# Untiled key products for two batches, a later remainder product in slab 5, and a value cast on VectorE in an attention-plus-MLP kernel

## Chip, cores, metric

One core of one Trainium2 chip. The metric is the device time of one execution in microseconds (us). A kernel's executions differ by some tenths of a per cent; every ratio here is between runs of the fast state (none over 1.5% above the fastest of its kernel), timed in the same rounds on the same chip as the kernel before. A profiled span is some 2 us shorter than the timed execution.

## The reference

Linear attention (softmax of q over the head dimension, softmax of k over the sequence), then a two-layer MLP with a swish whose slope is given per channel. It is 8 batches x 8 heads x 576 tokens x 64, so 4608 rows of 512, and an inner width of 2048.

```python
q_s = softmax(q, axis=-1);  k_s = softmax(k, axis=2)
kv  = einsum('bhsd,bhse->bhde', k_s, v)
x   = einsum('bhsd,bhde->bhse', q_s, kv)       # -> (B*S, H*D)
h   = x @ w_in                                 # 512 -> 2048
out = (h * sigmoid(beta * h)) @ w_out          # 2048 -> 512
```

## The kernel before

A hand-scheduled program. The rows go through in nine slabs of 512: slab b (0 to 7) holds the first 512 tokens of batch b, slab 8 the last 64 tokens ("remainder") of all batches. Each slab has a first pass (x times w_in, 64 matmuls of 512 columns) and a second (times w_out, 112 matmuls of 256 columns after a Strassen-like trick; 64 of 512 in slab 0). The attention of batch b + 1 is threaded between the matmuls of slab b. A counter of steps, 64 a pass, says where: `(step, work)`.

The parts that matter here:

```python
# key-value product of a head pair: column-tiled (two 64-column halves) or not
def tiled(b):
    return b > 1
...
if not tiled(b):
    mm(PS[bk][:, 256 * n:256 * n + VW - 1], l, r_[:, 0:VW - 1], j == 0, j == 4, ...)
for h in range(2) if tiled(b) else ():
    p = slice(64 * h, 64 * h + 64)
    add(PE, lambda e, h=h, p=p: e.matmul(PS[bk][p, ...], l[:, p], ..., tile_position=(0, 64 * h), ...))

# slabs 1 to 3 prepare batches 2 to 4 late in their second pass
def attn_late(b):
    ...
    if b < 4:
        s = [(101, steps(kv_all, b)), (104, lambda: g_diff(1))]
        return s + spread(x[0:2], 117, 120)      # output products: need QT

# queries: normalised on GpSimd, transposed by a DMA that SyncE issues
def norm_turn(b, hp0):  norm_main(b, hp0, 2, POOL); turn(b, hp0, 2)       # -> QT
def norm_turn_rem():    norm_rem(); turn_rem()                            # -> QTR

# remainder output products of slabs 4 to 6: need QTR
todo += spread(outr_steps(2 * t - 5), *((72, 88), (40, 56), (60, 76))[t - 4])

# batch 1, beside slab 0's second pass, in VectorE's order
norm_main(1, 2, 1, DVE)          # sums, reciprocal, multiply: EQ
w_sum(0, 4, 4)                   # half a weight sum: WSUM
norm_main(1, 3, 1, DVE)
w_sum(2, 4, 4)
```

Names in the profile: XT is x of a slab, GT its activations, GS sums of GT, EK and VB the exponentials of keys and the cast values, EKR those of the remainder keys, KVD the normalised key-value blocks (RC is the reciprocal in front of them). SPq is the queue of SyncE, which issues the transfers.

The softmax here doesn't subtract the row's maximum and nothing guards it: scores larger than these inputs give would overflow.

Of the kernel before, what the change touches and what calls it, by code (L numbers as in the profile page):

```python
# [8 lines left out]
ALU = mybir.AluOpType  # L9
AX = mybir.AxisListType  # L10
# [18 lines left out]
PE, ACTE, DVE, POOL, SP = "tensor", "scalar", "vector", "gpsimd", "sync"  # L29
# [13 lines left out]
class Program:  # L43
# [12 lines left out]
    def add(self, eng, fn, r=(), w=(), bank=(), slot=None, after=(), war=False):  # L56
        op = Op(eng, fn, slot)
        op.pos = len(self.ops)
        deps = op.deps
        deps.extend(after)  # L60
        for k in r:
            deps.extend(self.writer.get(k, ()))
            self.readers.setdefault(k, []).append(op)
        for k in w:
            for d in self.readers.get(k, ()):
                if d is not op and (war or not self._same(d, op)):
                    deps.append(d)
            for d in self.writer.get(k, ()):
                if not self._same(d, op):
                    deps.append(d)  # L70
            self.readers[k] = []
            self.writer[k] = [op]
        for k in bank:
            t = self.touch.setdefault(k, {})
            for e, d in t.items():
                if e != eng:
                    deps.append(d)
            t[eng] = op
        if eng == POOL and slot is None:
            if self.pool is not None:  # L80
                deps.append(self.pool)
            self.pool = op
        self.ops.append(op)
        return op
# [71 lines left out]
def bass_efficient_attn_shen__then__act_swish_beta_kernel(  # L156
# [12 lines left out]
    with ExitStack() as es:  # L169
        def sb(name, shape, dt):  # L170
# [52 lines left out]
        add = P.add  # L223
# [6 lines left out]
            r=["ts"], w=["idb"])  # L230
        add(POOL, lambda e: e.tensor_scalar(IDF[:, :], TS[0:NF, 0:NF], 0.0, None, ALU.is_equal),
            r=["ts"], w=["idf"])
        add(ACTE, lambda e: e.dma_start(BT[:, :], bass.AP(beta_h, 0, [[128, NF], [1, 128]])),
            w=["bt"], slot="bt")
        add(ACTE, lambda e: e.activation(DUMMY[:, 0:1], WARM[:, 0:1], ACT.Exp), r=["warm"],
            w=["dummy"])
# [91 lines left out]
            add(ACTE, lambda e: e.activation(EQR[:, :, :], QRF[:, :, :], ACT.Exp),  # L328
                r=[("qrf", 0), ("qrf", 1)], w=["eqr"])

        def norm_main(b, hp0, n, eng=DVE):
            i = b % 2
            a = bass.AP(EQ[i], hp0 * 512, [[2048, 128], [64, 8 * n], [1, 64]])
            s_ = bass.AP(QS[i], hp0 * 8, [[32, 128], [1, 8 * n]])
            v_ = bass.AP(QI[i], hp0 * 8, [[32, 128], [1, 8 * n]])
            vb = bass.AP(QI[i], hp0 * 8, [[32, 128], [1, 8 * n], [0, 64]])
            ks = [("eq", i, hp) for hp in range(hp0, hp0 + n)]
            add(DVE, lambda e: e.tensor_reduce(s_, a, AX.X, ALU.add), r=ks, w=[("qs", i, hp0)])  # L338
            add(DVE, lambda e: e.reciprocal(v_, s_), r=[("qs", i, hp0)], w=[("qi", i, hp0)])  # L339
            add(eng, lambda e: e.tensor_tensor(a, a, vb, ALU.mult), r=ks + [("qi", i, hp0)],  # L340
                w=ks)

        def norm_rem():
            vb = bass.AP(QRI, 0, [[H, 128], [1, H], [0, 64]])
# [77 lines left out]
            return b if b < 2 else 2 + b % 4  # L422

        def tiled(b):
            return b > 1

        def kvd(b, hp, bk, c):
            i = b % 2
# [52 lines left out]
        def outr_steps(b):  # L481
            pi = b // 2
            st = {}

            def one(hp, e_):
                if hp == 0 and e_ == 0:
                    st["b"] = bank()
                bk = st["b"]
                c = hp * 128 + e_ * 64
                d = kd(2 * pi + e_)  # L490
                mm(PS[bk][:, c:c + 64], KVD[d][:, hp, :], QTR[:, hp, 64 * e_:64 * e_ + 64],
                   True, True, r=[("kvd", d, hp), "qtr"], w=[("ps", bk)], bk=bk)
                if hp == 3 and e_ == 1:
                    o = bass.AP(XT8, pi * 128, [[NM * SM, 128], [SM, NM], [1, 128]])
                    add(DVE, lambda e: e.tensor_copy(o, PS[bk][:, :]), r=[("ps", bk)],
                        w=[("xt8", pi)], bank=[bk])
            return [lambda hp=hp, e_=e_: one(hp, e_) for hp in range(NHP) for e_ in range(2)]
# [22 lines left out]
        def one(fn, *a):  # L520
            return lambda: fn(*a)

        def steps(fn, *a):
            return lambda: go(fn(*a))
# [12 lines left out]
        def attn_late(b):  # L537
            x = []
            for hp in range(NHP):
                x += out_step(b, hp, MB, ACTE if hp % 2 else DVE)  # L540
            if b < 4:
                s = [(101, steps(kv_all, b)), (104, lambda: g_diff(1))]
                return s + spread(x[0:2], 117, 120)
            s = [(96, steps(kv_all, b)), (99, lambda: g_diff(1))]
            return s + spread(x, 107, 123)

        def spread(steps, lo, hi):
            return [(lo + (hi - lo) * k / len(steps), s) for k, s in enumerate(steps)]
# [29 lines left out]
        def load_wout(c):  # L578
# [11 lines left out]
            r=[("ps", bb)], w=["bc0"], bank=[bb])  # L590
        add(DVE, lambda e: e.scalar_tensor_tensor(BC[:, :], PS[bb][:, 0:NF], 1e-20, BC[:, :],
                                                  ALU.is_lt, ALU.mult),
            r=[("ps", bb), "bc0"], w=["bc"], bank=[bb])
# [120 lines left out]
        def g_diff(fh):  # L714
            f, th = NG * fh, 1 - fh
            add(DVE, lambda e: e.tensor_tensor(gv(f, th, NG), gv(f, th, NG), gv(f, 1 - th, NG),  # L716
                                               ALU.subtract),
                r=gk(f, 0, NG) + gk(f, 1, NG), w=gk(f, th, NG), war=True)
# [7 lines left out]
        def w_sum(n, i=0, k=NG):  # L726
            x, y = (((0, 0), (1, 1)), ((0, 0), (0, 1)), ((1, 0), (1, 1)))[n]
            add(DVE, lambda e: e.tensor_tensor(WSUM[n][:, i:i + k, :], quarter(*x)[:, i:i + k, :],  # L728
                                               quarter(*y)[:, i:i + k, :], ALU.add),
                r=wkeys(*x)[i:i + k] + wkeys(*y)[i:i + k],  # L730
                w=[("ws", n, i_) for i_ in range(i, i + k)])
# [127 lines left out]
        for t in range(NSLAB):  # L859
            todo = []  # L860
            if t == 0:
                todo = [(x, steps(t_steps, 1, (hp,), NOW, ACTE))
                        for hp, x in enumerate((97, 106, 114, 119))]
                todo += [(107, one(exp_kr_s, 1))]
                todo += [(x, one(exp_k, 1, hp, 1)) for hp, x in enumerate((108, 115, 120, 125.5))]
                todo += [(x, one(cast_v, 1, hp, DVE if hp else POOL))
                         for hp, x in enumerate((115, 118.5, 123, 127))]
                todo += [(x, steps(kv_steps, 1, (hp,), NOW))
                         for hp, x in enumerate((118, 122, 126))]
                todo += [(x, steps(out_step, 1, hp, NOW, ACTE)) for hp, x in enumerate((121, 125))]  # L870
                todo += [(117, one(o2_evac, 0, 0, 3, ACTE))]
                todo += [(2, steps(out_step, 0, 3, HEAD, DVE))]
            elif t < 4:
                todo = attn_late(t + 1)
                if t > 1:
                    todo += [(1, steps(out_step, t, 2, MB, ACTE)), (2.5, steps(out_step, t, 3))]
                if t == 3:
                    todo += [(4, one(norm_turn, 4, 2))]
                if t == 1:
                    todo += [(1, steps(out_step, 1, 2, (3,), ACTE)),  # L880
                             (3, steps(kv_steps, 1, (3,), (7,))),
                             (6, steps(out_step, 1, 3, (7,), DVE)),
                             (6.1, one(w_diff, 0)), (6.2, one(w_diff, 1))]
            elif t < 7:
                todo = attn(t + 1)
                if t > 3:
                    todo += spread(outr_steps(2 * t - 5), *((72, 88), (40, 56), (60, 76))[t - 4])
            elif t == 7:
                todo = spread(outr_steps(1), 32, 48)
            todo = sorted(todo, key=lambda x: -x[0])  # L890
# [30 lines left out]
            if t == 0:  # L921
                load_main("qf", qt_h, QF, 1, split=4, after=P.writer[("wout", 3, 0)])
                load_rem_s("krf", kt_h, KRF, 1)
                load_rem_s("vrf", vt_h, VRF, 1)
                load_kv(1)
                load(2, rem=False)
                exp_q(1)
                w_sum(0, 0, 4)
                w_sum(2, 0, 4)
                norm_main(1, 0, 1, DVE)  # L930
                norm_main(1, 1, 1, DVE)
                cast_vr_s(1)
                norm_main(1, 2, 1, DVE)
                w_sum(0, 4, 4)
                norm_main(1, 3, 1, DVE)
                w_sum(2, 4, 4)
                pass2_group(0, (0, 1, 2, 3), (3, 4, 5, 6), tick)
                while todo:
                    todo.pop()[1]()
                load(2, main=False)  # L940
                load_rem("qrf", qt_h, QRF, 2)
                add(ACTE, lambda e: e.activation(DUMMY[:, 2:3], WARM[:, 0:1], ACT.Silu),
                    r=["warm"], w=["dummy"])
                load(3)
                continue
# [95 lines left out]
```

## Time and profile before

| | before |
|---|---|
| time, median of 6 runs | 275.14 us (274.56 to 275.44) |
| span of the profiled run | 273.4 us |
| TensorE busy | 263.5 us (96%) |
| TensorE's clock | 0.997 |

To read it: "busy" of TensorE counts modelled matmul ends, so 96% does not mean 96% of its peak, but it does mean that TensorE nearly always has a matmul in hand. What is left to win by reordering is the list of its waits. A wait line names who waited, for which engine or transfer, how long in all, how often, and the longest. The lines are in the prediction.

### The profile page before, as it was taken

The numbers are of one execution on the slowest core, as the hardware profiler recorded it, in microseconds if no ns is written. First come the engines' busy times: TensorE is split into PE (matmuls) and PEld (weight loads), VectorE is DVE, ScalarE is ACT, GpSimd is POOL, SyncE is SP. The second block draws the span as 40 slices with busy tenths as digits, with TensorE's granted clock in tenths as the row PEclk, the third lists the DMA queues.
The fourth block names the chain that finished last, engine by engine and source line by source line (L and its number), as shares of the span: only waits on it lengthen the run. The fifth ranks groups of instructions, "written<-read, shape, count | busy, mean of one in ns | idle before, by whom it ended". The sixth has DMA issues, their size and how long they took to land.

```text
span 273.4 us, 4889 instructions
## 1 busy us (share of the span) xinstructions
PE 263.5 (96%) x1921; PEld 164.1 (60%) x1945; DVE 194.5 (71%) x415; ACT 181.0 (66%) x284; POOL 64.3 (24%) x81
## 2 busy tenths in 40 slices
PE   8899999999999999999999998999999999999994
PEld 3444454448744875478547863587458745874683
DVE  4964586787967799869786977778587549625762
ACT  4897568789288956897778846693783477018610
POOL 2790010006530099000900770036000100000000
PEclk9999999999999999999999999999999999999998
DMA  7999999989699139950499999303600030012005
GB/s 216 317 204 207 228 328 347 289 237 378 143 318 302 67 60 277 239 199 2 96 303 238 309 349 151 137 1 79 211 2 0 19 156 0 0 60 96 2 1 152
DMA packets 59366, 45.93 MB, mean 168 GB/s; under 512 B 28608, under 2 KB 58320, under 8 KB 58320
## 3 DMA queue, kind: packets, MB, share of 16 engines
q1 hardware_dynamic: 54480, 40.90, 53.2%
q0 software_dynamic: 4240, 4.19, 9.3%
q10 hardware_dynamic: 624, 0.53, 0.6%
q8 instruction: 15, 0.25, 0.4%
q14 instruction: 7, 0.06, 0.1%
HBM read 36.71 MB, written 9.44 MB: 169 GB/s over the span
## 4 chain that ended last, share of the span: by engine, by line
PE 70%; DMA 11%; DVE 7%; POOL 6%; SPq 2%; issue 2%; ACT 0%; POOLq 0%; DVEq 0%
PE PS L384 41%; PE PS L750 27%; DMA WOUT<-in_moe_w_out_dram 5%; POOL EQ L340 3%; DMA QF<-in_q_dram 3%; DMA QT<-EQ 2%; DVE QS L338 2%; SPq L503 2%; POOL WIN L574 1%; DVE GT L716 1%; DVE EQ L340 1%; POOL VB L355 1%; DMA QTR<-EQR 1%; PE PS L450 1%; DVE WSUM L728 1%
## 5 line engine op out<-in xcount | busy, mean ns | idle before, releaser
L384 PE MATMUL PS<-XT,WIN 128*128 128x512 bf16 x561 | 126.6, 379 | 1.2 <-issue 0.3
L650 ACT ACTIVATE GT<-PS,BETA 128x512 bf16<-128x512 f32 x144 | 95.1, 689 | 39.5 <-PE PS L384 39.3
L384 PEld LDWEIGHTS PS<-XT,WIN 128*128 128x128 bf16 x576 | 54.5, 98 | 63.6 <-DMA WIN<-in_moe_w_in_dram 0.7
L673 DVE TENSOR_SCALAR GT<-GT,RB 128x512 bf16<-128x512 bf16 x144 | 52.3, 384 | 37.8 <-ACT GT L650 36.9
L340 POOL TENSOR_TENSOR EQ<-EQ,QI 128x1024 bf16<-128x1024 bf16 (+1 forms) x13 | 25.6, 1966 | 46.7 <-DVE QI L339 46.0
L750 PE MATMUL PS<-WOUT,GS 128*128 128x256 bf16 x256 | 31.8, 273 | 0.2
L750 PE MATMUL PS<-WSUM,GT 128*128 128x256 bf16 x256 | 30.4, 273 | 1.0 <-DMA QT<-EQ 1.0
L750 PE MATMUL PS<-WOUT,GT 128*128 128x256 bf16 x256 | 30.9, 273 | 0.1
L750 PEld LDWEIGHTS PS<-WSUM,GT 128*128 128x128 bf16 x256 | 24.9, 98 | 3.9 <-issue 0.5
L750 PEld LDWEIGHTS PS<-WOUT,GT 128*128 128x128 bf16 x256 | 24.8, 98 | 3.7
L750 PEld LDWEIGHTS PS<-WOUT,GS 128*128 128x128 bf16 x256 | 24.5, 98 | 3.4
L786 ACT COPY O2S<-PS 128x512 f32<-128x512 f32 (+1 forms) x17 | 9.4, 560 | 24.4 <-PE PS L750 24.3
L355 POOL CAST VB<-VF 128x512 bf16<-128x512 f32 x25 | 17.1, 684 | 24.6 <-DVE GS L709 15.3
L307 ACT ACTIVATE EQ<-QF 128x512 bf16<-128x512 f32 x32 | 17.9, 619 | 7.3 <-DMA QF<-in_q_dram 7.2
L709 DVE TENSOR_TENSOR GS<-GT 128x512 bf16<-128x512 bf16 (+2 forms) x32 | 21.9, 685 | 0.0
L716 DVE TENSOR_TENSOR GT<-GT 128x2048 bf16<-128x2048 bf16 x16 | 20.4, 1302 | 0.0
L338 DVE TENSOR_REDUCE QS<-EQ 128x16 f32<-128x1024 bf16 (+1 forms) x20 | 19.8, 991 | 0.7 <-ACT EQ L307 0.7
L307 ACT ACTIVATE EK<-KF 128x512 bf16<-128x512 f32 x32 | 18.1, 620 | 0.1
L476 ACT CAST XT<-PS 128x512 bf16<-128x512 f32 x18 | 10.4, 581 | 11.7 <-PE PS L384 11.7
L798 DVE TENSOR_TENSOR O2S<-TS,PS 128x512 f32<-128x512 f32 (+1 forms) x17 | 10.7, 643 | 9.3 <-PE PS L750 9.3
L750 PE MATMUL PS<-WSUM,GS 128*128 128x256 bf16 x128 | 16.7, 273 | 0.0
L384 PE MATMUL PS<-WOUT,GT 128*128 128x512 bf16 x62 | 15.0, 379 | 0.1
(80 smaller groups left out, 219.8 us busy)
## 6 DMA issues: line engine op xcount, KB each, us to landing
out_dram<-O2S SPq DMA_DIRECT2D x8, 1024.0 KB, 5.2
QF<-in_q_dram SPq DMA_DIRECT2D x6, 1024.0 KB, 7.2
KF<-in_k_dram SPq DMA_DIRECT2D x6, 1024.0 KB, 9.6
VF<-in_v_dram SPq DMA_DIRECT2D x6, 1024.0 KB, 12.6
KF<-in_k_dram SPq DMA_DIRECT2D x8, 256.0 KB, 5.4
VF<-in_v_dram SPq DMA_DIRECT2D x8, 256.0 KB, 5.4
WOUT<-in_moe_w_out_dram POOLq DMA_DIRECT2D x4, 512.0 KB, 16.5
WIN<-in_moe_w_in_dram POOLq DMA_DIRECT2D x3, 512.0 KB, 9.4
```

The source lines that it names most:

```text
L307: add(ACTE, lambda e, o=o, a=a: e.activation(o, a, ACT.Exp), r=[(name + "f", i, hp)], w=[("e" + name, i, hp)])
L338: add(DVE, lambda e: e.tensor_reduce(s_, a, AX.X, ALU.add), r=ks, w=[("qs", i, hp0)])
L340: add(eng, lambda e: e.tensor_tensor(a, a, vb, ALU.mult), r=ks + [("qi", i, hp0)], w=ks)
L355: add(eng, lambda e: (e.copy if eng == ACTE else e.tensor_copy)(o, a), r=[("vf", i, hp), ("vone", i)], w=[("vb", i, hp)], after=after)
L384: add(PE, lambda e: e.matmul(o, l, r_, start=start, stop=stop), r=r, w=w, bank=[bk])
L476: add(eng, lambda e: (e.copy if eng == ACTE else e.tensor_copy)(XT[i][:, hp, :], PS[bk][:, :]), r=[("ps", bk)], w=[("xt", i, hp)], bank=[bk])
L650: add(ACTE, lambda e: e.activation(GT[:, f, :], PS[bk][:, :], ACT.Silu, scale=BETA[:, f:f + 1]), r=[("ps", bk), "beta"], w=[("gt", f, 0), ...
L673: add(DVE, lambda e: e.tensor_scalar(GT[:, f, :], GT[:, f, :], RB[:, f:f + 1], None, ALU.mult), r=k + ["rb"], w=k)
L709: add(DVE, lambda e: e.tensor_tensor(GS2[:, i:i + n, :], GT[:, i:i + n, :], GT[:, i + NG:i + NG + n, :], ALU.add), r=[k_ for f in (i, i + ...
L716: add(DVE, lambda e: e.tensor_tensor(gv(f, th, NG), gv(f, th, NG), gv(f, 1 - th, NG), ALU.subtract), r=gk(f, 0, NG) + gk(f, 1, NG), w=gk(f ...
L750: add(PE, lambda e, l=l, r_=r_, st=st, u=u, i=i, b_=b_: e.matmul(PS[b_][:, 256 * u:256 * u + 256], l, r_, start=st, stop=end and i == NG - ...
L798: add(DVE, lambda e, b_=b_, u0=u0, u1=u1: e.tensor_tensor(o[:, u0:u1, :], ts[:, u0:u1, :], bank3(b_)[:, u0:u1, :], ALU.add), r=["ts", ("ps ...
```

## The change

The intent as the code shows it: take TensorE's remaining waits away without new work. The remainder product of slab 5 goes to the second pass (part 1); batch 1's preparation on VectorE is reordered (part 2); the key products of batches 2 and 3 are no longer column-tiled and are spread between other matmuls (part 3). Left out of the listing below is the helper that splits the normalisation into its sums and its multiply.

```diff
         def tiled(b):
-            return b > 1
+            return b > 3
...
             if b < 4:
-                s = [(101, steps(kv_all, b)), (104, lambda: g_diff(1))]
+                s = spread(kv_steps(b, (0, 1)), 97, 101) + spread(kv_steps(b, (2, 3)), 101, 105)
+                s += [(105, lambda: g_diff(1))]
                 return s + spread(x[0:2], 117, 120)
...
-                todo += [(x, one(cast_v, 1, hp, DVE if hp else POOL))
-                         for hp, x in enumerate((115, 118.5, 123, 127))]
+                todo += [(x, one(cast_v, 1, hp, DVE))
+                         for hp, x in ((1, 118.5), (2, 123), (3, 127))]
...
-                todo += [(x, steps(out_step, 1, hp, NOW, ACTE)) for hp, x in enumerate((121, 125))]
+                todo += [(x, steps(out_step, 1, hp, NOW, ACTE)) for hp, x in enumerate((122.5, 125))]
...
-                             (6.1, one(w_diff, 0)), (6.2, one(w_diff, 1))]
+                             (6.1, one(w_sum, 2, 4, 4)), (6.2, one(w_diff, 0)),
+                             (6.3, one(w_diff, 1))]
...
-                    todo += spread(outr_steps(2 * t - 5), *((72, 88), (40, 56), (60, 76))[t - 4])
+                    todo += spread(outr_steps(2 * t - 5), *((72, 88), (72, 88), (60, 76))[t - 4])
...
+                norm_main(1, 3, 1, DVE, mult=False)
+                cast_v(1, 0, DVE)
+                norm_main(1, 3, 1, DVE, sums=False)
                 w_sum(0, 4, 4)
-                norm_main(1, 3, 1, DVE)
-                w_sum(2, 4, 4)
```

More of the change, by code (lines that the diff above doesn't have):

```diff
@@ L329, in exp_qr, with norm_main @@
                 r=[("qrf", 0), ("qrf", 1)], w=["eqr"])
-        def norm_main(b, hp0, n, eng=DVE):
+        def norm_main(b, hp0, n, eng=DVE, sums=True, mult=True):
             i = b % 2
@@ L337, in norm_main @@
             ks = [("eq", i, hp) for hp in range(hp0, hp0 + n)]
-            add(DVE, lambda e: e.tensor_reduce(s_, a, AX.X, ALU.add), r=ks, w=[("qs", i, hp0)])
-            add(DVE, lambda e: e.reciprocal(v_, s_), r=[("qs", i, hp0)], w=[("qi", i, hp0)])
-            add(eng, lambda e: e.tensor_tensor(a, a, vb, ALU.mult), r=ks + [("qi", i, hp0)],
-                w=ks)
+            if sums:
+                add(DVE, lambda e: e.tensor_reduce(s_, a, AX.X, ALU.add), r=ks,
+                    w=[("qs", i, hp0)])
+                add(DVE, lambda e: e.reciprocal(v_, s_), r=[("qs", i, hp0)], w=[("qi", i, hp0)])
+            if mult:
+                add(eng, lambda e: e.tensor_tensor(a, a, vb, ALU.mult), r=ks + [("qi", i, hp0)],
+                    w=ks)
         def norm_rem():
```

## The prediction

> **What bounds the kernel now.** I read the page's first two parts, then the list of waits, then TensorE's timeline in the three places that the diff touches, last the chain that ended last for the stretch in which batch 1 is prepared.
>
> The page says which engine to follow:
>
> ```profile
> PE 263.5 (96%) x1921; PEld 164.1 (60%) x1945; DVE 194.5 (71%) x415; ACT 181.0 (66%) x284; POOL 64.3 (24%) x81
> ...
> PEclk9999999999999999999999999999999999999998
> ```
>
> TensorE is busy for 263.5 of 273.4 us at full clock; no other engine passes 71%. So time can only come from TensorE's work getting shorter or from its few waits. The list of waits of TensorE (what waited, for what, us in total, times, longest) names them:
>
> ```profile
> PE PS L384 <- DMA QTR<-EQR: 1.2, 1, 1.2
> PE PS L750 <- DMA QT<-EQ: 1.0, 2, 0.5
> PE PS L382 <- DVE EQ L340: 0.8, 2, 0.4
> ...
> PE PS L384 <- DVE KVD L430: 0.2, 1, 0.2
> ```
>
> All four are touched by the change, directly or by what runs in front of them. Together 3.2 us, 1.2% of the span: this is about all that a reordering can win.
>
> The first wait, in TensorE's timeline (start, duration, engine, line, operation, count, idle before and releaser):
>
> ```profile
> 164.42 5.13 PE L384 MATMUL PS<-XT,WIN 128*128 128x512 bf16 x23 [0.16 <-issue]
> 170.72 0.20 PE L384 MATMUL PS<-QTR,KVD 128*128 128x64 bf16 x1 [1.18 <-DMA QTR<-EQR]
> 170.76 0.60 PE L384 MATMUL PS<-XT,WIN 128*128 128x512 bf16 x2
> ```
>
> The group of 23 spans 5.13 us and its last matmul 0.38, so starts are (5.13 - 0.38)/22 = 0.216 us apart, and the last starts at 169.17. The remainder product (QTR) would start at 169.39; it starts at 170.72, because the transposing transfer of the remainder queries has not landed. Counted in starts, 1.33 us are lost (the listed idle is less, as a matmul's modelled end lies some 0.16 us after the next may start).
>
> The second, with the column-tiled key block in front of it (slab 1; slab 2 looks alike):
>
> ```profile
> 66.54 2.02 PE L750 MATMUL PS<-WOUT,GT 128*128 128x256 bf16 x17
> 68.48 0.32 PE L450 MATMUL PS<-VB,EK 128*64 128x65 bf16 x8
> ...
> 69.11 0.20 PE L450 MATMUL PS<-VR,EKR 128*64 128x65 bf16 x2
> 69.24 1.81 PE L750 MATMUL PS<-WOUT,GT 128*128 128x256 bf16 x15
> 70.89 1.58 PE L750 MATMUL PS<-WSUM,GT 128*128 128x256 bf16 x13
> 73.01 0.49 PE L750 MATMUL PS<-WSUM,GT 128*128 128x256 bf16 x3 [0.54 <-DMA QT<-EQ]
> ```
>
> The 256-column matmuls start 0.109 us apart. Without the block the next would start at 68.40; it starts at 69.24, so the 40 tiled matmuls of a batch cost 0.84 us (0.85 in slab 2). The wait: one 512-column product of QT must stand between the 13 and the 3 (the instruction order has it, its record is missing, a matter of 0.22 us). It was due at 70.89 + 13 x 0.109 = 72.31 and came at 73.01 - 0.22 = 72.79: 0.48 us lost here, and by the same count 0.37 us in slab 2 (due 100.64, came 101.01).
>
> The third, in the chain of waits while batch 1 is prepared beside slab 0's second pass:
>
> ```profile
> 39.70 1.01 DVE WSUM L728
> 40.71 0.61 DVE QS L338
> ...
> 41.34 0.21 DVE QI L339
> ...
> 41.58 0.69 DVE EQ L340
> 42.27 0.60 DVE WSUM L728
> 42.87 0.09 DVE RC L458
> ...
> 42.99 0.36 DVE KVD L430
> ...
> 43.40 1.54 PE PS L384 x10
> ```
>
> Here VectorE sets the pace: two weight sums (WSUM) lie in front of what TensorE needs, the last normalised queries (EQ) and the first key-value block (KVD). TensorE's transposes of them, due at 41.95, start at 42.33 (0.38 lost), and the first output product, due at 43.00, at 43.40 (0.40 lost). The next three output products each lose 0.16 more, as a key product takes 1.10 us from its start over reciprocal and KVD on VectorE to its output product, and TensorE has only 0.94 us of other work in between.
>
> **What the Trainium skill says.**
> - "TensorEngine Tiling (Array Packing)", Key Properties, says that changing the tiling mode drains TensorE, and under Restrictions that column tiling excludes the fast weight load. The trace agrees with an edge cost: the 40 tiled starts spread over 0.65 us (68.48 to 69.13), the block costs 0.84, so some 0.19 us sit at its two ends.
> - "TensorE: Matmul & The Clock Gate", Back-to-back issue gap, gives N/2.4 + 2.5 ns: 57 ns for N = 131. The trace agrees: batch 1's untiled key products start 0.23 us before the fifth of their group (43.84 to 44.07), 58 ns each, weight loads hidden.
> - "VectorE: DVE Perf Modes", The perf-mode tier table, has a copy of fp32 in SBUF at twice the plain rate. The trace has VectorE's value cast at 0.42 us for 512 elements a lane, against 0.62 on GpSimd.
> - "GPSIMD Engine Reference", Specifications, says that GpSimd shares its SBUF interfaces with VectorE. The trace agrees: the WSUM at 39.62 takes 1.02 us from start to start while GpSimd casts VRS (39.26 to 40.17), 0.60 when GpSimd is still.
>
> **The change part by part.**
> (1) Slab 5's remainder product moves from steps 40 to 56 of its slab to steps 72 to 88, the place that it already has in slab 4, in the second pass. Its transfer lands at 170.67; the new place begins some 8 steps after the second pass starts (176.15 now, 174.8 without the wait). The wait goes, and the same 8 matmuls run 30 ns apart as before. VectorE's copy of the result (0.6 us from start to start) goes into the second pass too, between the same instructions as in slab 4, where TensorE shows no wait behind it. The next remainder transfer is issued after step 118, so it overwrites nothing still needed, and slab 6's use of it begins at step 60, far later. Worth: -1.33 us.
> (2) Batch 1: on VectorE, one WSUM (0.60) leaves for slab 1, and a cast (0.36 from start to start) comes in front of the EQ multiply. I walk it through. The sums of the last head pair follow EQ directly at 39.62 instead of 40.64; reciprocal at 40.34; the cast when its values have landed (GpSimd waited for them until 40.76), so 40.75 to 41.15; EQ multiply done by 41.8, so the transposes at 41.95 need not wait (0.38 won). WSUM 0.61, RC at 42.4, KVD, then the second value cast done by 43.25. In the new order TensorE runs the second key product in front of the first output product, due at 42.83; it waits for that cast until 43.3: 0.45 us lost, in place of 0.40. But with 1.16 us of TensorE work now between second key product and its output product, that one's 0.16 goes. Sum: (0.38 + 0.40 + 0.16) - 0.45 = 0.49 us won. The moved WSUM falls into slab 1's first pass, where VectorE has 0.20 + 0.71 + 0.22 + 0.44 us of idle between 52 and 56; nothing there is on the path.
> (3) Batches 2 and 3: 40 tiled matmuls become 20 untiled ones, spread between the 256-column ones. 20 x 0.0575 = 1.15 us instead of 0.84: +0.31 us each. In slab 1 the remainder keys may cost more: their exponential ends at 68.28 on ScalarE, the fifth step is due at 61.30 + 61 x 0.109 + 4 x 0.0575 = 68.19, so +0.14. These 0.45 (slab 1) and 0.31 us (slab 2) come in front of the QT waits of 0.48 and 0.37, and QT comes over VectorE, GpSimd and SyncE's transfer, none of which waits for a key product. They fill the waits, and the path gets 0. On VectorE the reciprocals do not wait: their second is reached at 71.2, the products end at about 70.5.
>
> Sum: -1.33 - 0.49 + 0 = -1.82 us on 275.08, 273.3 us.
>
> **The rivals.**
> (a) Filling is not exact: the spread key products cost more than 58 ns between matmuls of another shape, or the wait for the remainder keys is longer. Against it: 58 ns holds in slab 0 with matmuls of another size on both sides. For it: the margins are only 0.03 and 0.06 us. If each costs 30 ns more, 2 x 0.6 us would come back: 274.4.
> (b) In part 2 another wait takes the place: value transfers land one after another, and at 0.75 us per 256 KB (some 345 GB/s in that slice of the page) the second value lands around 42.3, half a microsecond before it is cast. If it is later, or the cast runs into GpSimd's VRS cast, part 2 wins 0 to 0.2: 273.7.
> (c) Slab 5's VectorE work in the second pass delays the sums' release of PSUM or the next norm. Slab 4 with the same order speaks against it; if so, half of part 1 is lost: 274.0.
> (d) Untiled blocks win where I see none, because the drain costs more than the starts show, or because the norm's transfer comes earlier: 272.6. I see nothing that makes QT earlier relative to its slab.
>
> **Range and chances.** The sum of known waits limits the gain to some 3 us, the cost in (a) to about 1 us. I predict 273.3 us, 8 in 10 between 272.5 and 274.4. Two per cent is 5.5 us, beyond every rival: within 2% at 0.97, faster by more 0.02, slower by more 0.01.
>
> **What would show it.** Part 1: the list of waits of TensorE without QTR, and slab 5's first pass some 1.3 us shorter. Part 2: the EQ wait in front of the transposes near zero, a new wait for a value cast (VB) of about 0.3 to 0.5 us, and slab 1's first pass starting about 0.5 us earlier. Part 3: no tiled matmuls before slab 3, QT waits shrunk to under 0.2 us, the length of slabs 1 and 2 unchanged. I am wrong if slabs 1 and 2 grow, if QTR still waits, or if the time before batch 1's first output product does not shrink.

## The result

| | before | after |
|---|---|---|
| time, median of 6 runs | 275.14 us | 273.56 us (273.04 to 273.95) |
| span of the profiled run | 273.4 us | 271.7 us |

The ratio is 0.9944, with a 95% interval from 0.9929 to 0.9958. Ratios here are the mean time of one kernel's runs over that of the other's runs of the same rounds, so not quite the ratio of the medians quoted. 1.58 us were won; 1.82 were predicted.

TensorE's list of waits after the change, the same view as in the prediction (its wait at the start of the kernel, two of unknown cause, and one of 0.2 us for GT that was there before, are left out):

```profile
PE PS L754 <- DMA QT<-EQ: 0.4, 1, 0.4
PE PS L385 <- DVE EQ L343: 0.4, 1, 0.4
...
PE PS L387 <- DVE VB L358: 0.3, 1, 0.3
```

The wait for QTR is gone, one of two for QT and one of two for EQ are gone (the EQ wait that stays is at 12 us, where the change does nothing), and a new wait of 0.3 us for a value cast VB has come. TensorE's timeline around slab 5's remainder product:

```profile
164.05 10.31 PE L387 MATMUL PS<-XT,WIN 128*128 128x512 bf16 x47 [0.16 <-issue]
174.19 1.47 PE L754 MATMUL PS<-WSUM,GS 128*128 128x256 bf16 x12
175.50 0.49 PE L754 MATMUL PS<-WOUT,GS 128*128 128x256 bf16 x3
175.83 0.19 PE L387 MATMUL PS<-QTR,KVD 128*128 128x64 bf16 x1
175.86 0.49 PE L754 MATMUL PS<-WOUT,GS 128*128 128x256 bf16 x3
```

The 47 matmuls now run without a gap, and each remainder product takes 0.03 us of the second pass from start to start. Slab 1's second pass, with the spread untiled products:

```profile
66.98 0.22 PE L387 MATMUL PS<-VB,EK 128*128 128x131 bf16 x1
67.04 0.27 PE L754 MATMUL PS<-WOUT,GT 128*128 128x256 bf16 x1
...
67.43 0.27 PE L754 MATMUL PS<-WOUT,GT 128*128 128x256 bf16 x1
67.69 0.23 PE L387 MATMUL PS<-VR,EKR 128*128 128x131 bf16 x1
...
70.70 1.58 PE L754 MATMUL PS<-WSUM,GT 128*128 128x256 bf16 x13
72.68 0.49 PE L754 MATMUL PS<-WSUM,GT 128*128 128x256 bf16 x3 [0.40 <-DMA QT<-EQ]
```

The first key product delays the next matmul by 0.06 us. The remainder key product (VR,EKR) comes 0.26 after the matmul at 67.43, where 0.11 would do: it waits 0.15 us for its exponential. And there is still a wait for QT in front of the three matmuls at 72.68. The chain of waits of batch 1's preparation:

```profile
40.58 0.43 DVE VB L358
41.01 0.60 DVE EQ L343
41.60 0.60 DVE WSUM L732
42.21 0.09 DVE RC L461
...
42.32 0.35 DVE KVD L433
42.67 0.34 DVE VB L358
...
43.15 2.68 PE PS L387 x19
```

One WSUM is left where two were, and TensorE goes on at 43.15 with the second key product.

Where the 1.7 us of the two spans come from, by the starts of the passes in TensorE's timelines (us):

| start of | before | after | gained up to there |
|---|---|---|---|
| slab 1, second pass | 61.30 | 60.65 | 0.65 (0.1 of it was there at 40 us, before any change took effect) |
| slab 2, first pass | 75.32 | 74.97 | 0.35 |
| slab 4, second pass | 146.56 | 146.20 | 0.36 |
| slab 5, second pass | 176.15 | 174.19 | 1.96 |
| slab 6, first pass | 189.45 | 187.73 | 1.72 |
| slab 8, first pass | 243.72 | 242.00 | 1.72 |

So 0.55 us come from batch 1, 0.30 are lost again at slab 1's QT, and 1.36 come from slab 5 (1.60 in its first pass, less 0.24 for the eight products that moved into the second). In slab 1 the transfer of QT took 3.53 us from issue to landing in place of 3.21; what goes with this is shown under "The whole change again".

### The profile page after: what moved, and what is told of

Read it like the earlier page. It is cut to its first block, busy times and chain, and to the rows that moved or that the text cites. A ratio compares the mean times of both kernels' runs of the same rounds, so it can differ in the third digit from the quotient of the medians.

```text
span 271.7 us, 4811 instructions
## 1 busy us (share of the span) xinstructions
PE 263.8 (97%) x1882; PEld 165.7 (61%) x1905; DVE 194.0 (71%) x416; ACT 181.0 (67%) x284; POOL 64.1 (24%) x80
## 4 chain that ended last, share of the span: by engine, by line
PE 85%; DVE 4%; DMA 4%; POOL 2%; SPq 2%; issue 2%; ACT 1%; POOLq 0%
PE PS L387 51%; PE PS L754 33%; DMA VF<-in_v_dram 2%; DMA QT<-EQ 1%; PE PS L453 1%; POOL VB L358 1%; SPq L275 1%; DVE QS L339 1%; SPq L287 1%; DVE EQ L343 1%; POOL EQ L343 1%; DVE VB L358 1%; ACT GT L654 1%; POOL VR L372 0%; DVE QI L341 0%
## 5 line engine op out<-in xcount | busy, mean ns | idle before, releaser
L387 PEld LDWEIGHTS PS<-XT,WIN 128*128 128x128 bf16 x576 | 55.2, 98 | 64.4 <-DVE XT L479 0.6
L754 PE MATMUL PS<-WOUT,GT 128*128 128x256 bf16 x256 | 33.0, 273 | 0.1
L754 PEld LDWEIGHTS PS<-WOUT,GS 128*128 128x128 bf16 x256 | 24.1, 98 | 3.4
```

The costliest lines, as they stand in the source:

```text
L387: add(PE, lambda e: e.matmul(o, l, r_, start=start, stop=stop), r=r, w=w, bank=[bk])
L754: add(PE, lambda e, l=l, r_=r_, st=st, u=u, i=i, b_=b_: e.matmul(PS[b_][:, 256 * u:256 * u + 256], l, r_, start=st, stop=end and i == NG - ...
```

## The experiments

Five timed rounds (4 to 6 runs of a kernel). All outputs are right. "us" is the median of the kernel's runs, "before" that of the kernel before on the same chip.

| kernel | us (lowest to highest) | before | ratio | 95% interval |
|---|---|---|---|---|
| part 1 alone | 273.82 (273.42 to 274.05) | 274.87 | 0.9956 | 0.9938 to 0.9975 |
| part 2 alone | 274.62 (274.02 to 275.45) | 274.87 | 0.9989 | 0.9966 to 1.0011 |
| part 3 alone | 273.96 (273.80 to 274.28) | 274.87 | 0.9964 | 0.9944 to 0.9985 |
| whole change again | 273.49 (273.29 to 274.36) | 274.87 | 0.9951 | 0.9930 to 0.9971 |
| change without part 3 | 273.47 (273.06 to 274.06) | 274.87 | 0.9946 | 0.9932 to 0.9960 |
| untiled in a burst | 273.58 (273.01 to 273.86) | 274.87 | 0.9951 | 0.9936 to 0.9965 |
| tiled and spread | 278.46 (278.19 to 278.75) | 274.87 | 1.0131 | 1.0115 to 1.0146 |
| nothing tiled | 274.81 (274.51 to 275.04) | 274.87 | 0.9997 | 0.9984 to 1.0010 |
| QT products later | 274.45 (274.13 to 274.55) | 274.97 | 0.9981 | 0.9966 to 0.9997 |
| second WSUM moved too | 273.34 (273.06 to 273.64) | 274.97 | 0.9943 | 0.9928 to 0.9959 |
| both of these | 274.02 (273.89 to 274.38) | 274.97 | 0.9967 | 0.9951 to 0.9984 |
| part 3 alone, padded | 275.31 (274.72 to 275.67) | 275.06 | 1.0004 | 0.9991 to 1.0017 |

My theory was that the change is a sum: a removed transfer wait (part 1), a shorter chain on VectorE (part 2), and key products that fill waits and so cost nothing (part 3). The rivals: part 3 changes QT's arrival, or its tiling saves more than the starts show; part 2's gain is eaten by a fixed arrival.

### Each part alone

**Part 1 alone.**

```diff
-    *((72, 88), (40, 56), (60, 76))[t - 4]
+    *((72, 88), (72, 88), (60, 76))[t - 4]
```

> Part 1 alone: the kernel before with slab 5's remainder product at steps 72 to 88. Theory (the whole change is the sum of a removed transfer wait, a shorter chain on VectorE, and key products that only fill waits): the wait for QTR goes and nothing takes its place, 1.3 to 1.4 us less than before (ratio 0.9952), slab 5's first pass 1.6 us shorter of which 0.24 us are the 8 moved products. Rival (a new wait in the second pass, for VectorE's copy): half of it, 0.6 to 0.7 us less (0.9976).

1.05 us by the medians, 1.2 by the ratio. The trace has no wait for QTR, and the time from slab 4's second pass to slab 5's fell from 29.59 to 28.00 us, which is 1.59 with 0.24 given to the moved products: 1.35 net, as worked out. That the timed gain is a little smaller may have a reason that comes up below: the wait for QTR is not the same in every execution.

**Part 2 alone.** The diff above without its first two hunks and without slab 5's steps.

> Part 2 alone: batch 1's first value cast on VectorE, one weight sum moved to slab 1, first output product later. Theory: 0.5 us less than before (ratio 0.998), with a wait for a value cast of about 0.3 us in place of those for the queries and for KVD. Rival (the gain is eaten by the wait for QT in slab 1, because QT's arrival is bound by something with a fixed time, such as loads): 0.0 to 0.2 us less (0.9995).

0.25 us by the medians, and the interval holds both 0 and the expected 0.5. The trace shows the mechanism: slab 1's second pass begins at 60.74 us instead of 61.30, but QT's transfer took 3.51 instead of 3.21 us, and at slab 2 0.27 us were left. This speaks for the rival: QT was issued 0.56 us earlier and landed only 0.26 us earlier (72.48 and 72.74), in both traces 1.35 to 1.38 us after the last packet of an older store (see "The whole change again"). Whether the gain always shrinks so, the timed runs are too noisy to say.

**Part 3 alone.** The first two hunks of the diff.

> Part 3 alone: untiled spread key products for batches 2 and 3. Theory: they cost 1.15 instead of 0.84 us a batch, and 0.15 more in slab 1, but lie in front of the waits for QT: within 0.1 us of before (ratio 1.000), waits for QT 0.03 to 0.1 us. Rival 1 (they delay QT by themselves, as slab 1's transfer in the changed kernel came 0.3 us later after its start than before): 0.3 us more (1.001) and a QT transfer of 3.5 us. Rival 2 (the drains of tiling cost more than the starts show): 0.3 us less or better (0.999).

0.91 us faster by the medians. All three guesses were wrong: theory and rival 1 plainly (QT's transfer took 3.16 us), and rival 2 in its reason. By the trace, slabs 1 and 2 did what the theory said: slab 4's second pass begins at 146.51 us, 0.05 before the kernel before, and the waits for QT are gone from the list. The gain is in slab 5, which this kernel does not touch: the wait for QTR is gone from the list too. From slab 4's second pass to slab 5's it is 28.48 us, so without the 0.24 of moved products only 0.24 us of the wait are left of 1.35. QTR comes earlier, though nothing in its own chain was changed. This is taken up below.

**The whole change again.**

> The whole change again, on the same chip and in the same rounds as its parts: 1.5 to 1.6 us less than before (ratio 0.9944), and the sum of the three parts if they are independent. If slab 1's QT transfer of 3.5 us was chance, it is 3.2 us here; if the change makes it, 3.5 again.

It gains 1.38 us by the medians, less than the sum of the parts (1.05 + 0.25 + 0.91 = 2.21): parts 1 and 3 both take away the same wait. In this trace there is no wait for QT at all: its product starts at 72.22 with QT issued at 68.98, so the transfer took at most 3.2 us. The 3.53 us of the first trace is therefore not a fixed price of the change; over all fourteen traces it lies between 3.14 and 3.85 us. The packets in these traces show what goes with it. Before QT, SyncE issues the store of slab 0's output (128 packets of 8 KB); in the trace of the result:

```profile
58.63 3.22 SPq L687 DMA_DIRECT2D out_dram<-O2S  x1
68.88 4.08 SPq L506 DMA_TRANSPOSE QT<-EQ  x2
```

The last of these packets ended at 71.02 us, and QT landed at 72.41. In nine traces that packet ended 1.8 to 2.5 us after QT's issue, and QT landed 1.35 to 1.39 us after it. In the other five it ended earlier, 0.8 to 1.6 us after the issue, and the transfer took 3.14 to 3.16 us. The kernel before is one of the nine (71.39 and 72.74). So the longer transfers of QT go with an older store that is still moving, and issuing QT earlier, as part 2 does, doesn't make that store end earlier. This is a reading of fourteen traces; no run moved the store.

### Part 3 within the change

**Without part 3.** Tiled bursts for batches 2 and 3 again, parts 1 and 2 kept.

> The changed kernel with part 3 undone (tiled bursts for batches 2 and 3 again): parts 1 and 2 together. Theory (key products lie in the waits for QT): the same as the changed kernel within 0.1 us (ratio to before 0.9944), the waits for QT back at 0.4 to 0.8 us. Rival (part 3 costs 0.3 us through a later QT): 0.3 us less than the changed kernel (0.9933).

273.47 us, as the changed kernel (273.49 and 273.56). It was run at another time. The rival's ratio, 0.9933, lies just inside the interval. Beside part 1, part 3 is worth nothing that shows; its trace has 0.9 us of waits for QT again, of which the untiled kernel's longer key products would fill a part.

**Untiled, in one burst.**

```diff
-    s = spread(kv_steps(b, (0, 1)), 97, 101) + spread(kv_steps(b, (2, 3)), 101, 105)
-    s += [(105, lambda: g_diff(1))]
+    s = [(101, steps(kv_all, b)), (104, lambda: g_diff(1))]
```

> The changed kernel with the untiled key products of batches 2 and 3 in one burst at step 101 instead of spread. Theory: spreading as such is worth nothing, as the sum of work in front of QT is the same; same as the changed kernel within 0.1 us (0.9944), and the 0.15 us wait for the remainder keys is gone. Rival (spreading helps VectorE to finish the KVD earlier): 0.2 us more than the changed kernel (0.9951).

273.58 us: spreading as such is worth nothing that shows. The ratio is the 0.9951 of the rival, but its interval (0.9936 to 0.9965) holds the theory's 0.9944 too, so the runs don't part the two. The wait for the remainder keys is gone from the trace, as the theory said.

**Tiled, but spread.** `tiled` back to `b > 1`, the steps 97 to 105 kept.

> The changed kernel with batches 2 and 3 tiled again but still spread, so that TensorE goes from full to tiled products and back some 15 times a slab. Theory (a tiled block pays at its two ends: 0.19 us of the 0.84 us in the trace of before): 15 x 0.19 + 0.65 = 3.5 us a slab instead of 1.15 to 1.3, less the waits for QT that are left: 3.5 to 4.5 us more than the changed kernel (277.5, ratio 1.009). Rival (the ends cost only because the burst is long): within 0.3 us of the changed kernel (0.9944).

278.46 us, 4.9 more than the burst, above even the 3.5 to 4.5 of the theory. TensorE's timeline shows what each change of tiling costs:

```profile
66.64 0.22 PE L453 MATMUL PS<-VB,EK 128*64 128x65 bf16 x2
66.80 0.28 PE L754 MATMUL PS<-WOUT,GT 128*128 128x256 bf16 x1
67.01 0.22 PE L453 MATMUL PS<-VB,EK 128*64 128x65 bf16 x2
67.16 0.28 PE L754 MATMUL PS<-WOUT,GT 128*128 128x256 bf16 x1
```

A full matmul follows two tiled ones after 0.16 us, and tiled ones follow it after 0.21, so a round takes 0.37 us where 0.11 + 2 x 0.016 would be its work. The key products spread from 66.53, where the next full matmul was due, to 72.08 (start of the eight matmuls behind them); less 14 matmuls of 0.109 in between, they cost 4.02 us a slab. Less 0.65 of work, that is 0.22 us for each of 15 tiled blocks. So the edges are real, the 0.19 us seen in the long burst was nearly the whole of it, and a tiled product pays only in a long burst.

**Nothing tiled.** `tiled` to `b > 7`.

> The changed kernel with no tiled key products at all, so also batches 4 to 7 untiled, where TensorE has no wait behind them. Theory: 0.31 us more a batch, 1.2 us more than the changed kernel (274.8, ratio 0.9989). Rival (the block's ends cost more than the starts show): no more than 0.2 us slower, or faster.

274.81 us, 1.23 more than the burst; 1.24 were worked out (4 x 0.31). Where no wait hides it, an untiled batch costs what the starts say.

### What is left

**QT's products later.**

```diff
-    return s + spread(x[0:2], 117, 120)
+    return s + spread(x[0:2], 121, 125)
```

> The changed kernel with the two output products of slabs 1 and 2 that wait for QT moved from steps 117 and 118.5 to 121 and 123. Theory (the wait for QT is the last thing left on the path there): its 0.34 us in slab 1 and 0.08 in slab 2 go, 0.4 us less than the changed kernel (272.9 to 273.2, ratio 0.993). Rival (the copies of their results on VectorE and ScalarE become late for the next slab's first products): 0 to 0.5 us more than the changed kernel, with waits of TensorE for XT.

274.45 us: slower than the changed kernel by 0.8 to 1.0 us if the ratios are compared (0.9981 with 0.9944 and 0.9951). They were run at other times. The same move costs 0.68 us where the second WSUM is moved too (274.02 and 273.34, below). The rival had the sign, not the wait. TensorE doesn't wait for QT, and for XT only 0.13 us in front of slab 3; it waits for GT:

```profile
PE PS L754 <- DVE GT L720: 0.8, 2, 0.5
```

```profile
99.35 1.91 PE L754 MATMUL PS<-WSUM,GT 128*128 128x256 bf16 x16
101.74 1.25 PE L754 MATMUL PS<-WSUM,GT 128*128 128x256 bf16 x8 [0.48 <-DVE GT L720]
```

The last 16 matmuls of the pass need a difference of GT that VectorE ends at 101.6. The two output products stood in front of them, and so did the wait for QT. Taken from there, they only uncover the next wait, and then have still to be run.

**The second WSUM moved too.** `w_sum(0, 4, 4)` also goes to slab 1, at step 6.05.

> The changed kernel with the other half weight sum (0.6 us) of batch 1's stretch moved to slab 1 as well. Theory (VectorE is what paces that stretch): the wait for the second value cast, 0.31 us, goes, 0.3 to 0.45 us less than the changed kernel (ratio 0.993). Rival (the transfers of the values pace it, since the first cast started as soon as they landed): a wait of VectorE for VF takes the place, under 0.15 us gained.

273.34 us; the wait for the value cast is gone from the list and none for VF has come, so the rival's wait did not come. By the ratios it gains 0 to 0.2 us on the changed kernel, inside the noise, so the timed gain of the theory (0.3 to 0.45) isn't confirmed; by the spans of the traces it is 0.5 and 0.7 (271.0 with 271.5 and 271.7).

**Both.**

> Both of these: if they are independent the sum, 0.7 to 0.8 us less than the changed kernel (272.7, ratio 0.9915).

274.02 us: the sum is not 0.8 us better but worse than the changed kernel, as the first of the two is. Against that one, the moved WSUM is worth 0.43 us by the medians, with intervals that overlap. In the trace with the moved WSUM alone the second key product starts at 42.77 us without a wait (43.15 in the changed kernel), but its slab 1's second pass begins at 60.27, no earlier than in one trace without the move (60.22, tiled and spread). No timed run shows a version that is clearly faster than the changed kernel.

### Why part 3 alone brings QTR earlier

QTR is issued by SyncE, which works through its transfers in order; issuing one can take it several us (6.20 us for two in the first row). Its rows from 138 us on, first of the kernel before, then of part 3 alone (start, time to issue; rows in between left out):

```profile
138.37 6.20 SPq L282 DMA_DIRECT2D KRF<-in_k_dram  x2
144.61 3.18 SPq L282 DMA_DIRECT2D VRF<-in_v_dram  x2
...
161.59 6.20 SPq L503 DMA_TRANSPOSE QT<-EQ  x2
168.24 1.19 SPq L510 DMA_TRANSPOSE QTR<-EQR  x1
```

```profile
138.50 4.93 SPq L282 DMA_DIRECT2D KRF<-in_k_dram  x2
143.47 2.92 SPq L282 DMA_DIRECT2D VRF<-in_v_dram  x2
...
159.77 6.75 SPq L503 DMA_TRANSPOSE QT<-EQ  x2
166.98 1.19 SPq L510 DMA_TRANSPOSE QTR<-EQR  x1
```

The loads of the next remainder keys (KRF) start at the same time and take 1.3 us less to issue; the transposing transfers follow 1.8 and QTR 1.3 us earlier. The lead isn't handed on row by row: among the rows left out, the next keys (KF) are issued at 151.29 and 151.15 us, and it is their landing that is 1.8 us earlier (162.85 and 161.03). Over all traces the issue of KRF parts cleanly: it takes 5.8 to 6.2 us in the five kernels that tile batches 2 and 3 (tiled and spread among them), and 4.9 to 5.3 us in the eight traces that do not. So it is not when the key products run, but that they are tiled, or that they are more: a tiled batch has 40 matmuls and as many weight loads, an untiled one 20. The queue of instruction transfers fits the second reading. Its line (packets, MB, share of 16 engines) in the window from 140 to 144 us of the kernel before

```profile
q8 instruction: 1, 0.02, 1.9%
```

is missing in that window of part 3 alone, where one falls between 146 and 150 us. 1.9% of 16 engines over 4 us is 1.2 us of one engine, in the midst of the loads that SyncE is issuing. In all five tiling kernels this 16 KB transfer falls into the issue of KRF (at 145.4 us in tiled and spread, where KRF starts at 142.6), in the eight others behind it (147.4 to 152.8 us). QTR itself parts less cleanly: counted from the start of slab 4's second pass it lands after 23.1 to 24.1 us in the five and 21.7 to 23.3 us in the eight, and the kernel before is the latest of the five, 1.0 us later than part 1 alone, which is the same program up to there. So a part of its 1.35 us of waiting is scatter.

**Part 3 alone, padded.** To tell the readings apart: keep the products untiled, but bring TensorE's count of instructions back by cutting the warm-up matmuls at the start into more, shorter ones.

```diff
-        warm(8, 0)
+        warm(28, 0, 146)
...
-        warm(10, 0)
+        warm(30, 0, 170)
```

> Part 3 alone again, but with 40 more and shorter warm-up matmuls at the start (18 of 512 columns become 58 of 146 or 170, about the same time), so that TensorE has issued as many instructions by slab 3 as in the kernel before. Open: part 3 alone gained 0.9 us although it was expected to gain none, because the remainder transfer of slab 5 came earlier; in all kernels with tiled products in slabs 1 and 2 the two transfers of remainder keys that SyncE issues in slab 3 take 5.8 to 6.2 us to issue, in all without them 4.9 to 5.3, and the one 16 KB transfer of the instruction queue falls into 140 to 144 us with them, into 146 to 149 us without. Theory (the number of TensorE instructions moves its instruction transfers against SyncE's data transfers): the issue takes 5.8 to 6.2 us again, TensorE waits 0.5 to 1.2 us for QTR again, 274.6 to 275.1 us (ratio to before 0.999 to 1.000). Rival (the tiled products themselves, or their time, do it): 5.0 us, a QTR wait under 0.3 us, and 273.9 to 274.1 us (ratio 0.9965).

275.31 us: the gain of part 3 alone is gone, with nothing changed but 40 more matmuls, all of them short, and their weight loads in the first 8 us. The two ratios' intervals don't overlap (0.9944 to 0.9985 and 0.9991 to 1.0017). The theory had the direction; issue, wait and time all came out somewhat above its ranges. SyncE and TensorE in this trace:

```profile
138.42 6.48 SPq L282 DMA_DIRECT2D KRF<-in_k_dram  x2
144.94 3.13 SPq L282 DMA_DIRECT2D VRF<-in_v_dram  x2
...
162.04 6.26 SPq L503 DMA_TRANSPOSE QT<-EQ  x2
168.76 1.19 SPq L510 DMA_TRANSPOSE QTR<-EQR  x1
```

```profile
PE PS L384 <- DMA QTR<-EQR: 1.7, 1, 1.7
```

The instruction transfer is back between 140 and 144 us. That the number of instructions ahead moves the time is shown by this pair; the tiling itself is ruled out as the cause. That it does so through the instruction transfer that takes an engine from SyncE's loads is the reading that fits every trace, but it is seen only as falling together in time: no run moved that transfer alone.

## Why the prediction was right, and where it was not

- **The total.** 1.82 us were predicted, 1.58 measured, inside the range. TensorE's list of waits did bound the gain. Part 1's 1.33 us rest on one trace of a wait that varies from kernel to kernel (next point), so that the total came out so near is luck in part.
- **Part 1, 1.33 us.** Confirmed: 1.35 us net in the trace of part 1 alone and 1.36 in the change, at no price in the second pass. What failed is the silent assumption that this wait is one number. By the same count over the traces with the product at steps 40 to 56 it is 1.35 us (before), 0.74 (part 2 alone), 0.24 (part 3 alone) and about 1.9 (padded).
- **Part 2, 0.49 us.** Its working held: the second key product started at 43.15 us (43.3 predicted), behind a wait of 0.31 us (0.45 predicted). Slab 1's second pass begins between 60.2 and 61.1 us, mean 60.73, in the eight traces with part 2 taken as it is, and between 61.2 and 61.35, mean 61.28, in the four without: 0.55 us. Timed alone it was 0.25 us and not clear of noise.
- **The EQ waits.** I counted both as touched by the change; one lies at 12 us and stayed. The walk used only the other, so the sum is not hurt.
- **Part 3, 0 us on the path.** Right beside part 1: the change without it is as fast. The terms were right too: 0.06 us a product, 0.15 us for the remainder keys (0.14 predicted; the two times it gives differ by 0.09, and the trace of the change has 0.06 us more from the end of the exponential, 67.63, to the matmul, 67.69), 0.31 us a batch where nothing hides it. "I see nothing that makes QT earlier" was true of QT, and missed QTR: alone, part 3 gains 0.9 us, because fewer instructions let SyncE issue the remainder transfer earlier. The prediction had no step for instruction transfers.
- **The missing 0.24 us.** The margin of 0.03 us that I gave slab 1's QT supposed that its transfer always takes 3.2 us. It took 3.53 us in the trace of the result, where the store of slab 0 was still moving until 71.02 us, and 0.34 us of waiting were left (due at 72.12, came at 72.46). By the reading of the fourteen traces, this is the step that the prediction lacked: it followed QT over VectorE, GpSimd and its own transfer, and not the older store in SyncE's queue. Rival (a) had the place, but not the size (1.2 us over two slabs; it was 0.30 us in one) and not the reason: the products cost what was said. The second trace of the change has no such wait, and yet its timed gain is 1.38 us; so the trace shows the 0.3 us, and the medians can't confirm it. Why the store ends now at 70.3 us and now at 71.5 stays open.
- **The cost of tiling.** Rival (d), that the drains cost more than the starts show, fell: 0.22 us for each tiled block when spread, 0.19 in the burst.

## What to carry to other kernels

In a kernel that keeps TensorE busy 96% of the time, read its list of waits, work out each in starts rather than idle time, and check what stands right behind a wait before taking it away: here the wait for QT hid one for GT. Column tiling pays in a burst (0.84 us a batch here, 1.15 untiled) and not between full products (4.02). And test each part alone and left out: a part can gain by moving something that it does not touch, such as when instructions are transferred, and such a gain is gone at the next edit.

## What the Trainium skill lacked or had wrong

- "TensorEngine Tiling (Array Packing)", Key Properties: it says that a change of tiling mode drains TensorE and gives no number. Here entering and leaving a tiled block cost 0.22 us together (15 blocks a slab), 0.19 us around a long burst.
- "TensorE: Matmul & The Clock Gate", Back-to-back issue gap: for streams of a weight load and a matmul each it gives 81 ns at N = 128 and 131 ns at N = 512, and says that its formula N/2.4 + 2.5 holds for an isolated matmul. Here the matmuls came with a weight load each (1921 matmuls and 1945 loads in the trace before, some matmul records missing), and the starts are 57 to 58 ns apart at 131 columns, 109 at 256 and 216 at 512, which is that formula.
- "Runtime: NRT & Kernel Launch", Instruction fetch mechanics: it says that instructions are refilled over DMA in blocks of 16 KiB, at a cost that is mostly hidden, and has no number for what this does to a kernel's own transfers. The trace has such transfers of 16 KB. Here 80 TensorE instructions more (p3 padded against part 3 alone) moved a transfer by SyncE from 166.98 to 168.76 us and the kernel from 273.96 to 275.31 us.
- No page that I read says how much a transposing transfer of the same size varies, or how long an older store holds one up: 3.14 to 3.85 us for the same QT in slab 1, the longer ones landing 1.35 to 1.39 us after the last packet of slab 0's store.
